# Batch 0's attention planned in halves of the heads, with its inputs in one row of the SyncE queue

## The chip, the cores and the metric

The kernel runs on one core of a Trainium2 chip. The metric is the device time of one execution in microseconds (us), the median of several runs. The engines are named as in the profile: PE (TensorE, with PEld for its weight loads), DVE (VectorE), ACT (ScalarE), POOL (GpSimd) and SP (SyncE, which only issues DMAs here).

## The reference

Two stages follow each other: a linear attention with cosine weights over 8 batches of 8 heads, 576 positions and 64 features, and a two-layer MLP with squared ReLU over the 4608 tokens that come out.

```python
# q, k, v: (8, 8, 576, 64) float32; w_in: (512, 2048); w_out: (2048, 512)
def phi(x, c, s):                     # c, s: cos and sin of pi/2 * pos / 576
    r = np.maximum(x, 0.0)
    return np.concatenate([r * c, r * s], axis=-1)
kv  = np.einsum('bhsf,bhsd->bhfd', phi(k), v)
z   = np.sum(phi(k), axis=2)
num = np.einsum('bhsf,bhfd->bhsd', phi(q), kv)
den = np.einsum('bhsf,bhf->bhs', phi(q), z)[..., None] + 1e-06
x   = (num / den).transpose(0, 2, 1, 3).reshape(4608, 512)
r   = np.maximum(x @ w_in, 0.0)
out = (r * r) @ w_out
```

## The kernel before

**Tiling.** A batch's 576 positions are four tiles of 128 (j = 0 to 3, the main part, with position p * 4 + j in row p) and a tail of 64. The tails of two batches share a tile, and the eight tails make a ninth block of 512 tokens for the MLP. All matmuls are in bf16. For one batch the attention does this: features of k (relu times cos, relu times sin, L320 on ACT or L324 on DVE), a cast of v into `vext` with a column of ones (L342, L344), the products of k and v summed over the tiles into `abank` (L366), a copy to `kvz` (L377); features of q, their transposes (L399 on PE, or a transposing DMA), a copy to `qpTp` (L407), the products with `kvz` (L418), a division in three DVE instructions (L436, L439, L442) into `x`, its transpose (L464 and the copy L468, or a DMA) into `xT`. The MLP's first matmul reads `xT` and `w1sb` into a PSUM bank, ACT takes the relu to `gT`, DVE squares it, and the second matmul reads `gT` and `w2sb`. Batches 0, 1 and 2 use plain products there (first matmul at L628 for batch 0, L487 and L503 for 1 and 2; second at L653 and L667), the later ones a form with seven products of halves instead of eight (L580, L766). `FIRST_7 = 3` says from which batch the first matmul has that form.

**Order.** Every instruction behind the opening is put into a `Plan`: an operation has an engine (or a choice of two), a cost, keys that it reads and writes, and a due time. `order` walks through modelled time, takes on each engine the ready operation with the earliest due time, and that order is the program. The table `SHIFTS` moves the due time of the operation with that number by so many microseconds. `plan.given` holds the times at which the plan takes data to be there.

**The opening before.** The opening is written out by hand ahead of the plan. SP issues the main part of k (1 MB). POOL issues k's tail, v (1 MB) and its tail, q in two pieces of two tiles each, and the four column blocks of w1, each cast from float32 (1 MB read) to bf16; a DMA that casts is issued on POOL. PE meanwhile runs 31 fillers on zeros (`warm`, L348). Then come k's features, v's casts, all products of k and v, one copy to `kvz`, tiles 0 and 1 of q through to `xT` with seven more fillers in the waits, q's features of tiles 2 and 3, and the loads for batch 1 (q, k, v) between the four blocks of w2, on POOL. The plan starts with the transposes of tiles 2 and 3 (L399 again). Batch 0's first matmul has eight parts: part s covers half s // 4 of the tokens (tiles 0 and 1, or 2 and 3) and column block s % 4 of w1, so parts 0 to 3 run through the four blocks for the first half, and 4 to 7 for the second.

Of the kernel before, what the change touches and what calls it, by code (L numbers as in the profile page):

```python
# [15 lines left out]
FP = 512  # L16
# [135 lines left out]
def kernel(  # L152
# [193 lines left out]
    def warm(n, banks):  # L346
        for i in range(n):
            nc.tensor.matmul(  # L348
                out=bank[banks[i % len(banks)]][:, :],
# [6 lines left out]
    def att_kv(b, js):  # L356
        vx, vxt = vexts[b % 2][0], vexts[b // 2 % 2][1]
        for j in js:
            for hh in range(HH):
                for half in range(2):  # L360
# [11 lines left out]
                    )  # L372

# [248 lines left out]
    def first_mm(s, step, a):  # L622
        half, hq = s // 4, s % 4
        for c in range(0, W, step):
            for i in (2 * a, 2 * a + 1):
                hb = hq * 4 + i
                for kb in range(KB):
                    nc.tensor.matmul(  # L628
                        out=bank[2 * (s % 2) + i // 2][:, i % 2 * W + c : i % 2 * W + c + step],
# [6 lines left out]
    def first_relu(s, a):  # L636
# [3 lines left out]
            in_=bank[2 * (s % 2) + a][:, :].rearrange("p (n c) -> p n c", n=2),  # L640
# [214 lines left out]
    def plan_q(b, j, cos=None, sin=None):  # L855
# [309 lines left out]
    for i, at in enumerate((16.4, 19.9, 22.6, 25.2)):  # L1165
        plan.given["w1", i] = at
# [29 lines left out]
    for s in range(8):  # L1196
        plan_first(s)
# [165 lines left out]
```

## Time and profile before

| what | us |
|---|---|
| median of 3 runs (lowest to highest) | 277.68 (277.61 to 278.15) |
| profiled execution, own time | 277.98 |
| its span, first to last instruction | 276.2 |
| PE busy (share of the span) | 265.8 (96%) |
| DVE busy | 216.5 (78%) |
| ACT busy | 186.4 (67%) |
| first matmul of batch 0's MLP (L628) | 19.67 |
| first matmul of batch 1's MLP (L487) | 54.26 |
| mean granted clock of PE | 0.996 |

The profile is one execution, so single durations belong to 277.98 us and not to the median. A PE that the profile calls busy need not run at its peak: the ends of matmuls are modelled. DMA rows are called q1 (issued on SP) and q0 (issued on POOL); all rows of a core share 16 DMA engines. A DMA share is the summed time of the packets over that of 16 engines, and goes over 1 in busy stretches.

### The profile page before, as it was taken

The page shows a single profiled execution, that of the slowest core. Times are in us where ns is not written, and L with a number is a line of the kernel's source. Part 1 is how long each engine was busy: PE and PEld are TensorE (multiplying, and loading weights), DVE is VectorE, ACT ScalarE, POOL GpSimd, SP SyncE. Part 2 cuts the span into 40 slices and gives each one's busy share as a digit, 9 for nine tenths or more (in the row PEclk, how much of TensorE's full clock was granted, in tenths as well). Part 3 has the DMA queues.
Part 4 walks back from the last instruction along what each step waited for, and adds up shares of the span by engine and source line. Part 5 has one row for each costly group of instructions (what it writes and reads, how often), then busy time and mean ns, then how long its engine had stood idle before and what let it go on. Part 6 is the DMA issues. An engine that isn't in the chain of part 4 may idle for free.

```text
span 276.2 us, 6556 instructions
## 1 busy us (share of the span) xinstructions
PE 265.8 (96%) x2651; PEld 210.5 (76%) x2659; DVE 216.5 (78%) x429; ACT 186.4 (67%) x334; POOL 19.3 (7%) x33
## 2 busy tenths in 40 slices
PE   8689999999999999999999999999999999999992
PEld 3368856665455459899888898999888888888882
DVE  1576695967965899799999998988999688967711
ACT  3575861796956698669998899957645665654131
POOL 8417100000000000000000000000000000000013
PEclk9999999999999999999999999999999999999998
DMA  7999998999999999998999999693033000300234
GB/s 210 319 207 278 311 253 268 291 219 351 225 253 282 252 214 217 316 304 197 245 283 236 261 264 326 118 232 103 14 59 128 26 4 0 141 13 2 81 112 114
DMA packets 83470, 53.38 MB, mean 193 GB/s; under 512 B 55888, under 2 KB 79824, under 8 KB 83440
## 3 DMA queue, kind: packets, MB, share of 16 engines
q1 hardware_dynamic: 77312, 42.28, 61.1%
q0 software_dynamic: 6048, 10.62, 16.3%
q8 instruction: 21, 0.34, 0.5%
q10 hardware_dynamic: 80, 0.07, 0.1%
q14 instruction: 9, 0.07, 0.1%
HBM read 36.70 MB, written 9.44 MB: 167 GB/s over the span
## 4 chain that ended last, share of the span: by engine, by line
PE 89%; DMA 3%; ACT 2%; DVE 2%; POOL 1%; issue 1%; POOLq 0%
PE bank L766 31%; PE bank L580 27%; PE bank L503 9%; PE bank L653 5%; PE bank L667 5%; PE bank L628 4%; PE abank L366 3%; PE abank L418 3%; DMA q<-in_q_dram 3%; ACT qp L320 1%; PE bank L399 1%; PE bank L487 1%; ACT gT L638 1%; DVE x L442 1%; PE bank L464 0%
## 5 line engine op out<-in xcount | busy, mean ns | idle before, releaser
L766 PEld LDWEIGHTS <-gT 128*128 128x128 bf16 x448 | 43.5, 98 | 5.1
L520 DVE TENSOR_TENSOR gT<-gT 128x2048 bf16<-128x2048 bf16 (+1 forms) x32 | 37.9, 1187 | 7.2 <-ACT gT L596 4.0
L766 PE MATMUL bank<-w2sb,gT 128*128 128x256 bf16 x336 | 42.2, 273 | 0.0
L580 PE MATMUL bank<-xT,w1sb 128*128 128x256 bf16 x288 | 41.1, 273 | 0.0
L580 PEld LDWEIGHTS <-w1sb 128*128 128x128 bf16 x384 | 36.9, 98 | 4.5
L596 ACT ACTIVATE gT<-bank 128x512 bf16<-128x512 f32 x48 | 28.8, 605 | 14.4 <-PE bank L580 14.1
L603 DVE TENSOR_TENSOR gT<-bank,qpTp 128x512 bf16<-128x512 f32 x48 | 31.0, 684 | 6.0 <-PE bank L580 5.9
L766 PEld LDWEIGHTS <-gs 128*128 128x128 bf16 x336 | 32.4, 98 | 3.7
L976 ACT COPY bank<-bank 128x512 f32<-128x512 f32 x48 | 27.9, 591 | 5.8 <-PE bank L580 5.2
L580 PEld LDWEIGHTS <-w1t 128*128 128x128 bf16 x288 | 27.7, 98 | 3.7
L580 PE MATMUL bank<-qpTp,w1t 128*128 128x256 bf16 x192 | 28.3, 273 | 0.0
L766 PE MATMUL bank<-w2t,gs 128*128 128x256 bf16 x224 | 28.2, 273 | 0.0
L503 PE MATMUL bank<-xT,w1sb 128*128 128x512 bf16 x116 | 27.7, 379 | 0.0
L512 ACT ACTIVATE gT<-bank 128x512 bf16<-128x512 f32 x32 | 18.6, 596 | 10.2 <-PE bank L503 10.1
L442 DVE TENSOR_TENSOR x<-abank,rden 128x512 bf16<-128x512 f32 x31 | 21.4, 692 | 1.1
L700 POOL DMA_DIRECT2D out_dram<-ysb x4 | 2.4, 615 | 239.6 <-ACT ysb L1068 236.7
L503 PEld LDWEIGHTS <-w1sb 128*128 128x128 bf16 x116 | 10.7, 98 | 11.0
L993 ACT COPY qpTp<-bank 128x512 f32<-128x512 f32 x24 | 14.0, 593 | 5.3 <-DVE x L442 2.5
L1064 DVE TENSOR_TENSOR ysb<-bank,y 128x512 f32<-128x512 f32 x14 | 9.6, 686 | 8.2 <-ACT y L1081 7.5
L320 ACT ACTIVATE kp<-k,sin_col 128x512 bf16<-128x512 f32 x21 | 14.6, 727 | 1.7 <-DMA k<-in_k_dram 1.7
L628 PE MATMUL bank<-xT,w1sb 128*128 128x256 bf16 (+1 forms) x160 | 15.4, 251 | 0.1
L436 DVE TENSOR_SCALAR den<-abank 128x8 f32<-128x8 f32 x35 | 5.6, 160 | 12.3 <-PE abank L418 12.3
(108 smaller groups left out, 445.7 us busy)
## 6 DMA issues: line engine op xcount, KB each, us to landing
out_dram<-ysb SPq DMA_DIRECT2D x16, 512.0 KB, 3.3
v<-in_v_dram SPq DMA_DIRECT2D x12, 512.0 KB, 7.2
q<-in_q_dram SPq DMA_DIRECT2D x12, 512.0 KB, 6.1
k<-in_k_dram SPq DMA_DIRECT2D x12, 512.0 KB, 6.5
v<-in_v_dram POOLq DMA_DIRECT2D x2, 1024.0 KB, 12.7
w1sb<-in_moe_w_in_dram POOLq DMA_DIRECT2D x4, 512.0 KB, 13.1
w2sb<-in_moe_w_out_dram POOLq DMA_DIRECT2D x4, 512.0 KB, 15.3
k<-in_k_dram SPq DMA_DIRECT2D x1, 1024.0 KB, 5.5
```

What stands on the lines that cost most here:

```text
L320: eng.activation(out=dst[ps, :, lo : lo + D], in_=src[ps], func=ACTF.Relu, scale=col[ps])
L442: nc.vector.tensor_tensor(out=x[:, a:z], in0=n4[:, :, :, 0:D].rearrange("p b (k l) d -> p b k l d", l=2), in1=rden[:, a:z] .rearrange("p b ...
L503: nc.tensor.matmul(out=out_, lhsT=w1sb[:, kb, hb * P : (hb + 1) * P], rhs=x_block(m, kb), start=(kb == 0), stop=(kb == KB - 1),)
L512: nc.scalar.activation(out=gT_of(m)[:, hb, :], in_=bank[to][:, :], func=ACTF.Relu)
L520: nc.vector.tensor_tensor(out=g, in0=g, in1=g, op=ALU.mult)
L580: nc.tensor.matmul(out=bank[to][:, s * W : (s + 1) * W], lhsT=lhs[:, kb, (2 * u + s) * P : (2 * u + s + 1) * P], rhs=rhs[:, kb, :], start= ...
L596: nc.scalar.activation(out=g_pair(m, i, j, u), in_=bank[to][:, :].rearrange("p (s c) -> p s c", s=2), func=ACTF.Relu,)
L603: nc.vector.tensor_tensor(out=g_pair(m, i, j, u), in0=bank[to][:, :].rearrange("p (s c) -> p s c", s=2), in1=in_five(u).rearrange("p (s c) ...
L628: nc.tensor.matmul(out=bank[2 * (s % 2) + i // 2][:, i % 2 * W + c : i % 2 * W + c + step], lhsT=w1sb[:, kb, hb * P : (hb + 1) * P], rhs=x ...
L766: nc.tensor.matmul(out=bank[to][:, s * DM2 : (s + 1) * DM2], lhsT=lhs[:, hb, s * P : (s + 1) * P], rhs=rhs[:, hb, :], start=(fresh and hb ...
L976: add("ACT", psum, lambda: nc.scalar.copy(out=bank[b][:, :], in_=bank[a][:, :]), r=[("bank", a)], w=[("bank", b)])
L993: add("ACT", psum, lambda u=u, Y=Y: nc.scalar.copy(out=in_five(u), in_=bank[Y][:, :]), r=[("bank", Y)], w=five)
```

## The change

The opening written by hand goes, and the plan now orders it. SP issues all of batch 0's inputs one behind the other: k, its tail, q's tiles 0 and 1, v's heads 0 to 3, v's tail, v's heads 4 to 7, q's tiles 2 and 3. On POOL a small copy out of v's first half (`gate`) stands ahead of the four w1 loads, so these are issued when that half has landed. The products of k and v, the copy to `kvz`, the products with q and the division of tiles 0 and 1 are done for heads 0 to 3 and heads 4 to 7 apart, each half in a bank of its own (`first_v`, `first_kv`, `first_kvz`, `first_num`, `first_div`). Batch 0's eight parts of the first matmul run in the order 0, 4, 1, 5, 2, 6, 3, 7. The fillers are 28 at the start and 10 single ones that the plan spreads; they write `abank` instead of banks 0 to 5. The table `SHIFTS` is another one, for the operations' new numbers. The few words that came with the change also name batch 2's first matmul as plain; no line of the diff speaks of it, and `FIRST_7` is 3 on both sides.

```diff
 SHIFTS = {
-    24: 2.4, 27: 4.4, 38: 2, 45: -2, 70: 2.6, 72: -12, 103: 8.6, 108: -11.2, 111: -8.8, 124: 1.2,
...
+    43: 1.2, 45: -4.2, 49: 2.2, 74: -0.2, 100: -1.6, 121: -1.2, 147: 3, 153: -2.6, 154: -5.4,
...
 }
...
+    def load_tiles(nm, b, eng, js):
+        kqv[nm, b] = main = home(inp, [P, H, J, D], nm, dtype=F32)
+        eng.dma_start(
+            out=main[:, :, js, :],
+            in_=src_of[nm][b, :, 0:MAIN, :].rearrange("h (p j) d -> p h j d", j=J)[:, :, js, :],
+        )
+
+    def gate():
+
+        got = home(const, [P, 1], "got", dtype=F32)
+        nc.gpsimd.tensor_copy(out=got[:, :], in_=kqv["v", 0][:, 0, 0, 0:1])
...
+    def first_kv(half, js):
+        vx, vxt = vexts[0]
+        for j in js:
+            for hh in range(HH):
+                h = half * HH + hh
+                if j < J:
+                    lhsT, rhs = kp_of(0, j)[:, h, :], vx[:, j, h, :]
+                else:
+                    lhsT, rhs = kp_of(0, j)[rows(0), h, :], vxt[rows(0), h, :]
+                nc.tensor.matmul(
+                    out=bank[4 + half][:, hh * E1 : (hh + 1) * E1],
...
+    def first_num(j, half):
+        for hh in range(HH):
+            nc.tensor.matmul(
+                out=bank[2 * j + half][:, hh * E1 : (hh + 1) * E1],
+                lhsT=qpTs[0, j][half][:, hh, :],
+                rhs=kvzs[0][:, half * HH + hh, :],
...
+    FIRST_S = (0, 4, 1, 5, 2, 6, 3, 7)
...
-    T0 = 16.8
-
-    for i, at in enumerate((16.4, 19.9, 22.6, 25.2)):
-        plan.given["w1", i] = at
+    T0, TM = 1.2, 15.4
+
+    for key, at in (
+        (("k", 0), 5.9), (("k", 1), 5.9), (("kt", 0), 6.3), (("q01",), 7.9), (("v", 0), 9.4),
+        (("vt", 0), 9.8), (("v", 1), 11.2),
+        (("q23",), 12.7),
+    ):
+        plan.given[key] = at
...
+    add("PE", 8.0, lambda: warm(28), w=[("T",)], due=0.0)
+    for i in range(10):
+        add("PE", 0.216, lambda: warm(1), w=[("T",)], due=20.0, after=9.2 + 0.5 * i)
+    add("POOL", 0.1, gate, r=[("v", 0)], due=0.0)
+    plan_pool(2.6, lambda: load_w1(0, 4), [("w1", 0)])
+    for i in range(1, 4):
+        plan_pool(2.6, lambda i=i: load_w1(i, 4), [("w1", i)])
...
-    for s in range(8):
+    for s in FIRST_S:
         plan_first(s)
...
     with tc.manual_schedule():
         load_main("k", 0, nc.sync)
-        load_tail("k", 0, nc.gpsimd)
-        load_main("v", 0, nc.gpsimd)
-        load_tail("v", 0, nc.gpsimd)
+        load_tail("k", 0, nc.sync)
+        load_tiles("q", 0, nc.sync, slice(0, 2))
+        load_half("v", 0, nc.sync, 0)
+        load_tail("v", 0, nc.sync)
+        load_half("v", 0, nc.sync, 1)
+        load_tiles("q", 0, nc.sync, slice(2, 4))
         constants()
-        load_main("q", 0, nc.gpsimd, 2)
-        warm(31, (0, 1, 2, 3))
...
         plan.run(T0)
```

More of the change, by code (lines that the diff above doesn't have):

```diff
@@ L344, in att_v, with warm @@
             copy(out=vexts[b // 2 % 2][1][ps, :, 0:D], in_=piece("v", b, j)[ps])
-    def warm(n, banks):
+    def warm(n):
         for i in range(n):
             nc.tensor.matmul(
-                out=bank[banks[i % len(banks)]][:, :],
+                out=abank[:, i % 2, :],
                 lhsT=zeros[:, 0:P],
@@ L372, in att_kv, with first_v @@
                     )
+    def first_v(half, js, eng):
+        hs = slice(half * HH, (half + 1) * HH)
+        copy = eng.copy if eng is nc.scalar else eng.tensor_copy
+        copy(
+            out=vexts[0][0][:, js, hs, 0:D],
+            in_=kqv["v", 0][:, hs, js, :].rearrange("p h j d -> p j h d"),
+        )
+    def first_kv(half, js):
[9 more added lines that the diff above has]
+                    out=bank[4 + half][:, hh * E1 : (hh + 1) * E1],
+                    lhsT=lhsT,
+                    rhs=rhs,
+                    start=(j == 0 and hh == 0),
+                    stop=(j == J and hh == HH - 1),
+                )
@@ new lines, in first_kvz @@
+    def first_kvz(half, eng):
+        kvzs[0] = home(att, [P, H, E1], "kvz", 0)
+        copy = eng.copy if eng is nc.scalar else eng.tensor_copy
+        copy(
+            out=kvzs[0][:, half * HH : (half + 1) * HH, :].rearrange("p h e -> p (h e)"),
+            in_=bank[4 + half][:, 0 : HH * E1],
+        )
+    def first_num(j, half):
[4 more added lines that the diff above has]
+                rhs=kvzs[0][:, half * HH + hh, :],
+                start=True,
+                stop=True,
+            )
@@ new lines @@
+    for j in range(2):
+        plan_q(0, j, src=[("q01",)])
+        plan_qT_pe(0, j, j, 10.0 + 0.3 * j, "DVE" if j == 0 else "ACT")
+    for half in range(2):
+        for i, e in enumerate(("DVE", "ACT")):
+            js = slice(2 * i, 2 * i + 2)
+            add(e, cost(e, FP, "cast"), lambda half=half, js=js, e=e: first_v(half, js, ENG[e]),
+                r=[("v", half)], w=[("v0", half, i)])
+        if half == 0:
+            plan_v(0, J)
+        for js, r in (
+            (range(J), [("v0", half, i) for i in range(2)] + [("kp", j, x) for j in range(J) for x in "cs"]),
+            ((J,), [("kpt", 0, "c"), ("kpt", 0, "s"), ("vt", 0, 0)]),
+        ):
+            add("PE", 0.135 * len(js), lambda half=half, js=js: first_kv(half, js), r=r, w=[("bank", 4 + half)],
+                due=11.0 + half)
+        add_either(260, "psum", lambda e, half=half: first_kvz(half, e), [("bank", 4 + half)], [("kvz", 0, half)])
@@ L1191 @@
+    for j in range(2):
+        for half in range(2):
+            add("PE", 0.14, lambda j=j, half=half: first_num(j, half), r=[where[0, j], ("kvz", 0, half)],
+                w=[("bank", 2 * j + half)], due=12.5 + 0.3 * j)
+            add("DVE", 0.65, lambda j=j, half=half: first_div(j, half), r=[("bank", 2 * j + half)], w=[("x", j)])
+        plan_x_pe(0, j, 4 + j, TM - 0.5 + 0.9 * j, "ACT")
     for j in (2, 3):
-        plan_qT_pe(0, j, 4 + j % 2, T0 + 1.0 + 0.4 * (j - 2), "DVE" if j == 2 else "ACT")
+        plan_q(0, j, src=[("q23",)])
+        plan_qT_pe(0, j, 4 + j % 2, TM - 1.0 + 0.4 * (j - 2), "DVE" if j == 2 else "ACT")
@@ L1193 @@
+    for i in range(2):
+        add("PE", 0.0, lambda: None, r=[("kvz", 0, i)], w=[("kvz", 0)])
     for j in (2, 3):
-        plan_num(0, j, T0 + 3.0 + 1.6 * (j - 2))
-        plan_x_pe(0, j, 4 + j % 2, T0 + 5.0 + 1.6 * (j - 2), "DVE")
-    for s in range(8):
+        plan_num(0, j, TM + 0.5 + 0.8 * (j - 2))
+        plan_x_pe(0, j, 4 + j % 2, TM + 1.8 + 0.8 * (j - 2), "DVE")
+    plan_pool(2.6, lambda: load_main("q", 1, nc.gpsimd), [("q", 0), ("q", 1), ("q01",), ("q23",)])
+    plan_pool(2.6, lambda: load_w2(0, 4), [("w2", 0)])
```

104 lines of the change are left out of this document (45 added, 59 removed), and 63 rows, old and new, of the table SHIFTS.

## The prediction, made before the changed kernel was run

> **What bounds the kernel now.** I read the page first, then busy time by stage, then the order of time of the first 55 us, then the DMA rows.
>
> ```profile
> span 276.2 us, 6556 instructions
> ...
> PE 265.8 (96%) x2651; PEld 210.5 (76%) x2659; DVE 216.5 (78%) x429; ACT 186.4 (67%) x334; POOL 19.3 (7%) x33
> ```
>
> TensorE is the engine that fills the span. By stage (columns: stretch, its length, busy time and count on each engine, granted clock, DMA share, GB/s):
>
> ```profile
> 0.00:6.40 6.40, 5.20 (x17) 2.08 (x18) 0.51 (x6) 1.71 (x4) 5.04 (x14) 1.00 0.71 209
> 6.40:12.20 5.80, 3.26 (x16) 1.37 (x14) 2.78 (x7) 3.60 (x6) 3.59 (x5) 1.00 0.98 330
> 12.20:19.60 7.40, 6.48 (x102) 4.91 (x103) 6.34 (x19) 5.07 (x9) 0.02 (x1) 1.00 1.23 217
> ...
> 54.00:271.20 217.20, 216.99 (x2154) 177.05 (x2156) 181.98 (x343) 154.91 (x282) 2.52 (x5) 1.00 0.72 175
> ```
>
> From 54 us on PE is busy 216.99 of 217.20 us at a clock of 1.00: no order of that work can save more than 0.2 us. The time to be had lies before PE's dense stream, whose first real matmul is the first one of L628. In order of time:
>
> ```profile
> 11.74 1.10 DVE L342 CAST vext<-v 128x512 bf16<-128x512 f32 x3 [3.02 <-DMA v<-in_v_dram]
> 12.23 1.13 PE L366 MATMUL abank<-vext,kp 128*128 128x65 bf16 x32 [2.57 <-DVE vext L342]
> ...
> 18.78 1.05 PE L399 MATMUL bank<-ident,qp 128*128 128x128 bf16 x16 [0.20 <-DVE qp L324]
> ...
> 19.67 1.06 PE L628 MATMUL bank<-xT,w1sb 128*128 128x128 bf16 x16
> ...
> 24.18 0.41 DVE L468 COPY xT<-bank 128x512 bf16<-128x512 bf16 x1
> ...
> 24.75 0.43 DVE L468 COPY xT<-bank 128x512 bf16<-128x512 bf16 x1 [0.16 <-PE bank L464]
> ```
>
> Batch 0's k is there at 6.37 us, but v's casts wait until 11.74 and PE's first product with them. The stream begins at 19.67 and ends at 271.1; 5.1 us of last copies and stores follow, which the change leaves alone. The DMA rows (packets, MB, share of the 16 engines): first 5.0 to 5.75 us, where both rows run, then 44.5 to 49.5 us, where the SyncE row runs alone.
>
> ```profile
> q0 software_dynamic: 49, 0.16, 81.4%
> q1 hardware_dynamic: 134, 0.12, 46.7%
> ```
> ```profile
> DMA packets 2002, 1.91 MB, mean 381 GB/s; under 512 B 169, under 2 KB 2002, under 8 KB 2002
> ...
> q1 hardware_dynamic: 2002, 1.91, 108.8%
> ```
>
> Alone, the SyncE row moves 381 GB/s. Between 5.5 and 7.0 us, where the GpSimd row takes over from it, the stage table gives 234 GB/s. The first chunk of w1, issued at 6.64, lands 10.6 us later (the w1sb tile's own view), at 17.26; the next ones each 2.5 to 2.6 us after (0.5 MB in bf16, 1 MB read).
>
> **Part by part. (1) The inputs in one SyncE row.** Seven issues take 0.4 to 1.0 us each on SP (rows of the later loads: half of v 0.4 to 1.0, vt 0.7 to 1.1), all before their data's turn. k lands as now, 5.5 us after 0.74, at 6.2. Behind it come, at 381 GB/s, kt 0.13 MB, q's tiles 0-1 0.52, half of v 0.52, vt 0.13, the other half 0.52, q's tiles 2-3 0.52: landings at 6.6, 7.9, 9.3, 9.7, 11.0 and 12.4. q's pieces are now 512 B long, and no row shows such pieces on this queue; by the 234 GB/s of the handover v's second half would land at 14.0, as late as q now. I take 11.0 to 12.0: the long stretch alone on the row is nearest. Today v lands at 11.7 and q's first tiles at 13.4, so q's features leave the critical place and v's halves take it.
>
> **(2) The gate and w1.** A copy of 128x1 on GpSimd (0.10 us, as its constants) waits for v's first half; queued behind it on GpSimd are all four w1 loads and after them q1, w2, k1 and v1. w1's first issue goes from 6.64 to about 9.4. That costs nothing while the input row keeps the DMA engines full (until about 11.5, 0.9 before the last landing); without that cover it would cost the idle time between, up to 2 us. With the engines never idle, w1's first chunk ends 2.6 us after the inputs: 15.0. Unchanged it would be 17.26. Both are the bounds.
>
> The Trainium skill (Trainium Kernel Development and Optimization, Key Constraints) says that the DMAs of all issuing queues run on the same 16 engines, and that spreading them saves issue time alone. By it the same bytes end when they did, w1 stays at 17.26, and the gain below shrinks by 0.9 us. The rates of 234 and 381 GB/s in this trace speak against a plain sum of bytes.
>
> **(3) The chain in halves.** From v's second half: cast 0.62 (ACT), 20 products (half of 1.13 + 0.41 us) 0.8, kvz half of 0.69, four products 0.2, division 0.1 + 0.20 + 0.38, transposes 0.39, ACT copy 0.58: 3.6 us, and six hand-overs of 0.2: 4.8. Landing at 11.0 to 12.0 gives xT's first tile at 15.8 to 16.8. DVE and ACT together: features of five k tiles and two q tiles at 0.48 + 0.71, casts 2.5, kvz 0.7, copies of qT 1.7, divisions 2.7, copies of xT 1.2: 17.1 us on two engines, from 6.3, so not before 14.9. Of weights (15.0 to 17.3), chain and load the middle of the first two decides: I take 16.5 for the first matmul of L628, against 19.67. Gain 3.17.
>
> **(4) What slides behind the start.** The sixteen transposes of q's tiles 2-3 at 18.78 ran before the stream, and now within it: 0.90 lost. The products and transposes of tiles 2-3 were already within it.
>
> **(5) The new order of the first matmul, 0, 4, 1, 5...** Part 0 is 32 matmuls of 56 ns, 1.8 us, to 18.3; transposes and products of tile 2 carry PE to 19.5. Part 4 needs xT of tile 2, part 1 w1's second chunk (17.6 at the earliest, 19.86 as now). Tile 2, from q's last landing: features 0.71, transposes 0.61, copy 0.69, products 0.41, division 1.06, transposes 0.39, copy 0.41: 4.3, and seven hand-overs of 0.2: 5.7. q's last piece (12.4 alone) shares the DMA engines with w1: at equal shares 13.8. So tile 2 is there at 19.5 and tile 3 some 1.3 later, while the first half of part 4 lasts 0.9. Bounds: nothing, if part 1 fills it, to 4 us (rival D). I take 0.9, less the 0.40 gap that PE has now at 23.8: 0.5 lost. In return each w1 chunk serves two parts, 3.7 us of PE against 2.6 us of DMA, so later chunks are not waited for.
>
> **(6) Warm-up, table, the rest.** 31 + 8 fillers become 28 + 10, all in time in which PE waits (2.57 us before L366): nothing, and if they came late, 0.2 us each on the chain. The clock stayed at 1.00 through that wait. The new table reorders everything behind; PE's 0.2 us of slack bounds its gain, 1.5 us (a wait like the longest now, 2.57, once, half covered) its loss; I take nothing. Supply behind: w2's first chunk lands at 30.5 and is used at 35.0, batch 2's xT lands at 74.0 and is used at 76.5; a stream 1.8 us earlier stays inside. "Batch 2's first matmul plain" is no part of the diff: FIRST_7 is 3 on both sides. Nothing.
>
> **Sum.** The profiled execution took 277.98 (span 276.2 and 1.78 around it): -3.17 + 0.90 + 0.50 = -1.77, so 276.2; the median of the runs is 0.30 lower: 275.9. My case runs from 275.0 to 277.0 (start 15.6 to 17.6).
>
> **Rivals.** B, everything packs: first matmul at 15.6, no new gap and the 0.40 one gone: -4.07 + 0.90 - 0.40, 274.1. For it: PE's stream has work enough. Against: DVE and ACT would have to be full from 6.3 on.
>
> C, given back: the same bytes end when they do now (what the Key Constraints quoted above would give). w1's first chunk stays at 17.26, the start gains 2.3 only, and batch 1's inputs come no earlier (v1 lands at 39.3 now, its xT serves PE at 54.3), since the GpSimd row already runs without pause (DMA share 1.15 from 19.6 to 35). PE starts early and waits before batch 1's first matmul: 277.7. Against: the faster row, above; w2 and v1 follow w1.
>
> D, slower: the second half of xT comes late. Today q's last piece lands at 14.8, and its xT copies end at 24.6 and 25.2, 9.8 us later. Behind part 0 nothing hides this any more: from 13.8 it gives 23.6, PE stands from 19.5 for 4.1 us: -3.17 + 0.90 + 4.1 = +1.8, 279.5. It decides from 21.8 on. Against: now nobody is in a hurry for them.
>
> E, q's last piece starved: if rows took turns packet by packet, its 64 packets of 512 B on each engine would each wait for one of the other row (means from the page's DMA table: 16.3% and 61.1% of 16 x 276.2 us over 6048 and 77312 packets, 119 and 35 ns): 9.9 us from its turn at 10.1, landing at 20.9, tile 2 at 26.6, PE 7.1 late: 282.5. Such turns are what the Trainium skill describes (DMA: Bandwidth & Descriptors, Queues, rings and completion order: round-robin between rows by packet). The trace agrees in part: at 5.0 to 5.75 us the SyncE row got 134 packets to 49, about equal bytes.
>
> **Numbers.** About 0.2% (0.56 us) is what a measurement of this kernel tells from no change. My case 0.53, B 0.13: faster 0.66. C 0.11: same. D 0.17 and E 0.06: slower 0.23. The range, 273.9 to 279.6, takes in B, C and D and leaves out E and the ends.
>
> **What would show it.** First matmul of L628's form at 16 to 17; v's casts at 9.4 and 11.2; w1's first landing at 15 to 16.5; a gap under 1 us before xT's second half; L503's first use 1 to 3 us earlier than 55.1; PE full from there. Wrong, if the first matmul is early and the first use of L503 is not, or if PE stands over 2 us after part 0.

## The result, and the profile after

The changed kernel takes 282.76 us (median of 4 runs, 281.76 to 283.02), the kernel before on the same chip 277.81: ratio 1.017 (1.0143 to 1.0198). It is slower by 4.95 us, where 1.8 less had been forecast. Run again beside another set of runs of before it took 281.13 against 277.24: 1.0147 (1.0101 to 1.0194). The two profiled executions (282.87 and 277.98) differ by 4.9 us, and 3.6 of these lie in the span; the time around the span was 3.07 us instead of 1.78 in that execution and 1.81 when the kernel was run again, so 1.3 us of this difference are no matter of the order of work.

From the page of the changed kernel:

```profile
span 279.8 us, 6568 instructions
...
PE 268.1 (96%) x2651; PEld 210.8 (75%) x2658; DVE 223.0 (80%) x446; ACT 179.2 (64%) x320; POOL 15.4 (6%) x29
...
PE 74%; DMA 15%; issue 4%; DVE 2%; ACT 1%; POOL 1%; POOLq 0%; SPq 0%; ACTq 0%
```

The last line is the chain that ended last, by engine. In the kernel before it is 89% PE and 3% DMA. So over some seventh of the span the work that ended last is now traced back to transfers, while PE itself is as busy as before beside them (96%). The stage table says where (same columns as for before):

```profile
0.00:6.40 6.40, 5.21 (x13) 1.90 (x14) 0.51 (x6) 1.68 (x3) 1.04 (x9) 1.00 0.75 199
6.40:12.20 5.80, 5.40 (x49) 2.92 (x48) 3.77 (x9) 4.82 (x8) 0.90 (x2) 1.00 1.16 244
12.20:19.60 7.40, 5.21 (x71) 3.38 (x70) 5.58 (x18) 4.06 (x7) 4.32 (x7) 1.00 1.21 240
19.60:35.00 15.40, 15.27 (x202) 14.03 (x200) 10.65 (x22) 10.49 (x18) 5.62 (x7) 1.00 1.18 264
35.00:54.00 19.00, 17.74 (x166) 10.73 (x167) 14.14 (x33) 7.22 (x13) 0.00 (x0) 1.00 1.13 289
```

From 6.4 to 12.2 us the DMA engines are busier than before (1.16 against 0.98) and move less (244 GB/s against 330). From 35 to 54 us PE stands 1.26 us, before 0.26. The milestones, read from the order of time ("run again" is the changed kernel's second profiled execution, of 280.91 us):

| start of | before | after | later by | run again |
|---|---|---|---|---|
| first matmul of batch 0's MLP (L628, now L702) | 19.67 | 20.38 | 0.71 | 19.68 |
| first matmul of batch 1's (L487, now L558) | 54.26 | 55.82 | 1.56 | 55.24 |
| first matmul of L580's form, now L651 | 97.55 | 98.75 | 1.20 | 98.07 |
| the last matmul | 271.03 | 274.62 | 3.59 | 274.01 |

So the opening is late by 0.7 us where 3.2 less had been forecast, and the dense stream behind it is 2.9 us longer. Run again, the kernel started level with before, and its stream was as long (254.3 us): the longer stream is the loss that both executions show, and the gain of the start is missing in both. The landings, against what the forecast said:

| tile | before | forecast | after | run again |
|---|---|---|---|---|
| k's tail | 6.92 | 6.6 | 7.83 | 7.53 |
| q's tiles 0-1 | 13.42 | 7.9 | 9.36 | 9.15 |
| v's first half | 11.72 | 9.3 | 11.25 | 11.18 |
| v's tail | 12.44 | 9.7 | 12.36 | 11.81 |
| v's second half | 11.72 | 11.0 to 12.0 | 13.69 | 13.20 |
| q's tiles 2-3 | 14.80 | 12.4 to 13.8 | 15.44 | 14.91 |
| w1, first chunk | 17.26 | 15.0 | 17.75 | 17.54 |
| batch 1's v | 39.27 | "follows w1" | 42.35 | 41.76 |

The second half of v decides over the chain, and it comes 1.97 us later than the whole of v did before. (In the other runs below with before's queues and with the tails the whole of v landed at 10.82 to 11.31, so 11.72 is late for these queues.) The row as SP issues it (start, duration):

```profile
2.71 2.25 SPq L229 DMA_DIRECT2D v<-in_v_dram  x1
5.00 1.25 SPq L239 DMA_DIRECT2D vt<-in_v_dram  x1
6.29 1.05 SPq L229 DMA_DIRECT2D v<-in_v_dram  x1
7.39 0.93 SPq L216 DMA_DIRECT2D q<-in_q_dram  x1
```

and stretches of one microsecond on the DMA engines (the last two numbers of a row are DMA share and GB/s):

```profile
6.00:7.00 1.00, 1.00 (x5) 0.36 (x4) 0.21 (x1) 0.24 (x1) 0.00 (x0) 1.00 1.28 159
...
9.00:10.00 1.00, 1.00 (x5) 0.29 (x3) 0.86 (x3) 0.94 (x2) 0.00 (x0) 1.00 1.11 336
...
11.00:12.00 1.00, 0.69 (x16) 0.56 (x14) 0.43 (x1) 0.73 (x2) 0.70 (x2) 1.00 1.09 162
```

One issue took 2.25 us (the prediction had 0.4 to 1.0 for its like), but all are out by 8.3. The rate falls to 159 and 162 GB/s around the tails: k's lands 1.15 us behind k (7.83 - 6.68) and v's 1.11 behind v's first half, 0.13 MB each, which at 381 GB/s is 0.34. In between the row reaches 336. The packets from 10 to 11 us, and then from 11 to 12, tell more exactly what is slow:

```profile
DMA packets 524, 0.23 MB, mean 228 GB/s; under 512 B 394, under 2 KB 524, under 8 KB 524
...
DMA packets 158, 0.16 MB, mean 162 GB/s; under 512 B 0, under 2 KB 158, under 8 KB 158
```

The tail's 256 B pieces move for the most part in the first stretch. The lowest rate is in the second, which has none of them: there the pieces of v's second half behind the tail take 110 ns each (a share of 1.09 over 16 engines for 1 us, by 158). So a tail costs less by its own pieces than by what happens to those behind it.

Then the chain, in order of time:

```profile
13.71 0.62 ACT L388 CAST vext<-v 128x512 bf16<-128x512 f32 x1 [0.91 <-DMA v<-in_v_dram]
13.71 0.64 DVE L388 CAST vext<-v 128x512 bf16<-128x512 f32 x1 [0.31 <-DMA v<-in_v_dram]
14.27 0.41 DVE L413 CAST kvz<-bank 128x260 bf16<-128x260 f32 x1
14.73 0.41 PE L420 MATMUL bank<-kvz,qpTp 128*128 128x65 bf16 x8 [0.40 <-DVE kvz L413]
...
14.99 0.67 PE L402 MATMUL bank<-vext,kp 128*128 128x65 bf16 x16
...
16.55 0.42 DVE L413 CAST kvz<-bank 128x260 bf16<-128x260 f32 x1
...
18.24 0.40 PE L535 MATMUL bank<-ident,x 128*128 128x128 bf16 x4 [0.69 <-DVE x L435]
...
18.56 0.59 ACT L539 COPY xT<-bank 128x512 bf16<-128x512 bf16 x1 [1.15 <-PE bank L535]
...
19.20 1.34 PE L470 MATMUL bank<-ident,qp 128*128 128x128 bf16 x16
19.30 0.59 ACT L539 COPY xT<-bank 128x512 bf16<-128x512 bf16 x1 [0.15 <-PE bank L535]
...
20.38 0.39 PE L702 MATMUL bank<-xT,w1sb 128*128 128x128 bf16 x4
```

Half 0 gains little on half 1. Its products with v ended at 13.1, but its copy to `kvz` (14.27) stands on DVE behind the cast of half 1 (13.71), which waits for its DMA; half 1's products with v (14.99) stand on PE behind half 0's with q; half 1's copy (16.55) stands on DVE behind both divisions of half 0; and PE does the sixteen transposes of q's tiles 2-3 before the MLP's first matmul, as the kernel before did. From landing to first matmul: 6.7 us.

What waits later shows in the chain that ended last (start, duration, what) and, below it, in the order of time:

```profile
12.58 8.60 DMA w1sb<-in_moe_w_in_dram
21.90 20.45 DMA v<-in_v_dram
...
103.99 4.80 DMA qptT<-qpt
```
```profile
43.05 1.13 PE L377 MATMUL abank<-vext,kp 128*128 128x65 bf16 x32 [0.70 <-ACT vext L353]
```
```profile
130.38 0.43 DVE L633 TENSOR_TENSOR qpTp<-xT 128x512 bf16<-128x512 bf16 x1 [1.70 <-DMA xT<-x]
130.84 0.42 DVE L633 TENSOR_TENSOR qpTp<-xT,qpTp 128x512 bf16<-128x512 bf16 x1
130.86 0.60 PE L651 MATMUL bank<-qpTp,w1t 128*128 128x256 bf16 x4 [0.73 <-DVE qpTp L633]
```

Batch 1's v, last but a few on GpSimd's row, lands at 42.35, is cast, and PE stands for it. PE also stands at 108.8 (0.37 us for a transposing DMA) and at 130 (for `xT`, which another transposing DMA brings). From 104 to 140 us PE is busy 34.73 of 36.00 us at a DMA share of 1.16; before, 36.00 of 36.00 at 1.07. Whether these later waits are the inputs' lateness handed on, or come from transfers that are slower in themselves, is not shown.

### The profile page after: what moved, and what is told of

Its sections match the earlier page's. It is cut to its first block, busy times and chain, and to the rows that moved or that the text cites. A ratio compares the mean times of both kernels' runs of the same rounds, so it can differ in the third digit from the quotient of the medians.

```text
span 279.8 us, 6568 instructions
## 1 busy us (share of the span) xinstructions
PE 268.1 (96%) x2651; PEld 210.8 (75%) x2658; DVE 223.0 (80%) x446; ACT 179.2 (64%) x320; POOL 15.4 (6%) x29
## 4 chain that ended last, share of the span: by engine, by line
PE 74%; DMA 15%; issue 4%; DVE 2%; ACT 1%; POOL 1%; POOLq 0%; SPq 0%; ACTq 0%
PE bank L840 28%; PE bank L651 24%; DMA v<-in_v_dram 7%; PE bank L574 7%; PE bank L741 5%; PE bank L727 3%; DMA w1sb<-in_moe_w_in_dram 3%; PE abank L489 3%; PE abank L377 3%; DMA out_dram<-ysb 2%; DMA qptT<-qpt 2%; DMA vt<-in_v_dram 2%; PE bank L558 1%; ACT vext L353 1%; DVE gs L819 1%
## 5 line engine op out<-in xcount | busy, mean ns | idle before, releaser
L651 PE MATMUL bank<-xT,w1sb 128*128 128x256 bf16 x288 | 41.5, 273 | 0.0
L667 ACT ACTIVATE gT<-bank 128x512 bf16<-128x512 f32 x48 | 28.5, 609 | 19.7 <-PE bank L651 15.1
L651 PEld LDWEIGHTS <-w1sb 128*128 128x128 bf16 x384 | 36.5, 98 | 4.9 <-issue 0.3
L651 PEld LDWEIGHTS <-w1t 128*128 128x128 bf16 x288 | 27.8, 98 | 4.5 <-issue 0.9
L651 PE MATMUL bank<-qpTp,w1t 128*128 128x256 bf16 x192 | 28.0, 272 | 0.7 <-DVE qpTp L633 0.7
L583 ACT ACTIVATE gT<-bank 128x512 bf16<-128x512 f32 x32 | 18.3, 604 | 9.1 <-PE bank L574 9.1
L513 DVE TENSOR_TENSOR x<-abank,rden 128x512 bf16<-128x512 f32 x30 | 20.8, 692 | 1.0
L702 PE MATMUL bank<-xT,w1sb 128*128 128x256 bf16 (+1 forms) x160 | 15.5, 251 | 0.0
L727 PE MATMUL bank<-w2sb,gT 128*128 128x512 bf16 x61 | 15.0, 379 | 0.3 <-issue 0.2
L741 PE MATMUL bank<-w2sb,gT 128*128 128x512 bf16 x61 | 14.5, 379 | 0.2
## 6 DMA issues: line engine op xcount, KB each, us to landing
q<-in_q_dram POOLq DMA_DIRECT2D x1, 1024.0 KB, 11.5
```

The costliest lines, as they stand in the source:

```text
L513: nc.vector.tensor_tensor(out=x[:, a:z], in0=n4[:, :, :, 0:D].rearrange("p b (k l) d -> p b k l d", l=2), in1=rden[:, a:z] .rearrange("p b ...
L583: nc.scalar.activation(out=gT_of(m)[:, hb, :], in_=bank[to][:, :], func=ACTF.Relu)
L651: nc.tensor.matmul(out=bank[to][:, s * W : (s + 1) * W], lhsT=lhs[:, kb, (2 * u + s) * P : (2 * u + s + 1) * P], rhs=rhs[:, kb, :], start= ...
L667: nc.scalar.activation(out=g_pair(m, i, j, u), in_=bank[to][:, :].rearrange("p (s c) -> p s c", s=2), func=ACTF.Relu,)
L702: nc.tensor.matmul(out=bank[2 * (FIRST_S.index(s) % 2) + i // 2][:, i % 2 * W + c : i % 2 * W + c + step], lhsT=w1sb[:, kb, hb * P : (hb + ...
L727: nc.tensor.matmul(out=bank[FIRST_Y[tt]][:, :], lhsT=gT_of(0)[:, hb, tt * P : (tt + 1) * P], rhs=w2sb[:, hb, :], start=(hb == 0), stop=(hb ...
```

## The experiments

Each run was compared with runs of the kernel before on the same chip (medians 277.2 to 277.8). "Start" is the first matmul of batch 0's MLP, "stream" from there to the last matmul's start, in the profile; before has 19.67 and 251.4, the changed kernel 20.38 and 254.2 (run again 19.68 and 254.3). One kernel's start can differ by 0.7 us or more, then, and each "start" below is that of one execution.

**Inputs and plan apart.** Two kernels cross the parts: the change with before's input queues, and before with the new row and gate.

```diff
 # a_inputs_old: the changed kernel, with
-        load_tail("k", 0, nc.sync)
-        load_tiles("q", 0, nc.sync, slice(0, 2))
...
+        load_tail("k", 0, nc.gpsimd)
+        load_main("v", 0, nc.gpsimd)
+        load_tail("v", 0, nc.gpsimd)
...
+        load_main("q", 0, nc.gpsimd, 2)
-    add("POOL", 0.1, gate, r=[("v", 0)], due=0.0)
+    add("POOL", 0.1, lambda: None, r=[("v", 0)], due=0.0)
```

> The changed kernel with batch 0's inputs issued as before (k on SP; the tails, v and q in two pieces on GpSimd ahead of w1; the gate's place in the plan kept, without its copy). Plan, halves and table stay. Theory R (the row delivers late, and the loads behind the gate with it): w1's first chunk lands near 17.3 instead of 17.75 and v of batch 1 near 39.5 instead of 42.35, and the time falls from 282.8 to 278 to 280. Theory T (the order behind, with its new table, loses the time whatever the inputs do): 282 to 284, because the plan counts on q at 7.9 and v at 9.4, and now both come later.

> The kernel before with the change's input row alone: the seven loads in the row's order on SP, and the gate ahead of w1. Hand-written opening, order and table stay. Theory R: w1's chunks land some 1.5 us later and v of batch 1 some 3 us later, so 280 to 282. Theory T: within 0.6 us of 277.8, since v's and q's data come no later than PE's first use of them.

Measured: 282.29 (ratio 1.0178, 1.0162 to 1.0193) and 286.78 (1.0334, 1.0305 to 1.0364). The first is where theory T had it, the second beyond both theories. From the waits of PE (us in total, times, longest), the first kernel, then the second:

```profile
PE bank L470 <- ACT qp L331: 4.3, 1, 4.3
```
```profile
PE abank L378 <- DVE vext L354: 4.0, 1, 4.0
PE bank L592 <- DVE qpTp L574: 3.6, 2, 2.7
```

The changed plan takes q first; with the old queues q lands at 12.88, PE stands 4.3 us for it, and the stream starts at 24.74. The order before takes v first; with the new row v's second half lands at 13.43, and the stream starts at 22.41. Order and landing times belong together, so neither half alone says what it costs within the whole. One thing is seen all the same: where the start is as late as 24.74 the stream is dense, 251.0 us, as before's 251.4. The 2.9 us by which it is longer in the changed kernel are not work added to the stream; started 4 to 5 us earlier, it waits.

**The gate.** The copy that holds w1 back is left out.

```diff
-    add("POOL", 0.1, gate, r=[("v", 0)], due=0.0)
+    add("POOL", 0.1, lambda: None, r=[("v", 0)], due=0.0)
```

> The changed kernel without the gate's copy: w1's four loads are issued on GpSimd from about 2 us on and share the DMA engines with the row. Theory R in the form that the gate holds the GpSimd row back too long: w1's last chunk lands 1 to 2 us earlier than 26.5, v of batch 1 as well, 280 to 281.5. If the row itself is the cost (small pieces, 1.1 us for each tail), the sum of the bytes is unchanged, inputs come later by as much as w1 comes earlier: 283 to 286. Theory T: no change beyond 0.6 us.

Measured: 289.38 (1.0438, 1.0411 to 1.0465), start 31.61. This is beyond both ranges of the expectation. w1's first chunk lands at 11.71 and v's second half at 23.85 instead of 13.69. From 12 to 17 us both rows got equally many packets (packets, MB, share):

```profile
q0 software_dynamic: 671, 0.67, 78.8%
q1 hardware_dynamic: 668, 0.49, 40.2%
```

The rows take turns packet by packet, and the row with the smaller pieces moves less: this is rival E's mechanism, at the row that the gate protects. The stream behind the late start is dense again (251.0 us), so the loss is that of the start. This kernel needs the gate.

**The table.** `SHIFTS = {}` in the changed kernel, the same in before, and the changed kernel in the old order of parts (`FIRST_S = (0, 1, 2, 3, 4, 5, 6, 7)`) without table.

> The changed kernel with an empty table of order. Theory T says that this table is of no use or of harm at these arrival times: 281 to 284. If the table does its work and the loss is the row's, taking it away costs what such a table is worth: 285 to 290.

> The kernel before with an empty table of order, to set beside the changed one without its table (285.8, 3 to 4.7 us more than with it). If the change's structure is no worse and only its table fits less well: 286 to 290 here, so the table before was worth 9 us or more. If the structure is what costs: 281 to 283, about as much table gain as in the changed kernel.

> The changed kernel without its table and with the parts of the first matmul in their old order 0 to 7, so that the two orders are compared with no table that fits one of them. If the new order of parts is a gain (w1's chunks are asked for half as fast): 0.5 to 2 us slower than 285.8. If it costs, because part 4 waits for the second half of xT: 1 to 2 us faster.

Measured: 285.79 (1.032, 1.0287 to 1.0354), 279.59 (1.0073, 1.0045 to 1.0101) and 285.25 (1.0287, 1.0229 to 1.0344). The new table is worth 3.0 to 4.7 us to the changed kernel (against its two medians), the old one 2.3 to before, which is less than either case of the expectation. So the table is not the cause; it covers part of it. Without tables the difference is 6.2 us. The order of parts makes no difference that these intervals show.

**The tails, and the form of the row.** The changed kernel again as it is; with k's and v's tails of batch 0 issued on GpSimd; and, on top of that, q whole in its first half's place.

```diff
 # a_tails_pool
-        load_tail("k", 0, nc.sync)
+        load_tail("k", 0, nc.gpsimd)
...
-        load_tail("v", 0, nc.sync)
+        load_tail("v", 0, nc.gpsimd)
 # a_row_big, also
-        load_tiles("q", 0, nc.sync, slice(0, 2))
+        load_main("q", 0, nc.sync)
...
-        load_tiles("q", 0, nc.sync, slice(2, 4))
```

> The changed kernel once more, beside the next three on one chip. If its 282.8 is the program's, 281.5 to 283 and the same landings as in its first profile to 0.5 us: v's second half at 13.7, w1's last chunk at 26.5, v of batch 1 at 42.3. If the slow spells of the DMA engines in its first profile (33 and 39 to 40 us) were an accident of that execution, v of batch 1 lands near 40.5 and the time is 280 to 281.

> The changed kernel with the two tails of k and v issued on GpSimd (as before), all else in the row. If pieces of 256 B in the row are what makes the inputs late (1.1 us a tail against 0.34 by bytes), v's second half lands 1.5 us earlier, at 12.2, the GpSimd row after it as well, and the time is 280 to 281. If the row's bytes set the landings whatever the pieces, within 0.6 us of the changed kernel.

> The changed kernel with no small pieces in the row: tails on GpSimd, and q in one load of 1 KB pieces in the place of its first half, v's halves behind it. By 381 GB/s v's second half lands at 11.5 to 12; with it the time is 279.5 to 280.5 if late inputs and a late GpSimd row are the loss. If the plan's order is, its DVE order is still the same and v's first half now comes later: 282 to 284.

Measured: 281.13, 283.22 (1.0211, 1.0178 to 1.0243) and 282.66 (1.0209, 1.0168 to 1.025). The second is slower than both cases of its expectation, the third is where it was expected if the plan's order costs. v's second half landed at 13.20, 13.64 and 15.57, and the stream started at 19.68, 21.84 and 24.62. Beside the row the tails cost as much as within it: from 6 to 10 us the engines moved 182 GB/s. So it isn't the place in the queue that makes a tail dear. In the second kernel something else came in; its rows of 18 to 21 and 21.5 to 24.5 us (PE busy second, granted clock third from the end):

```profile
18.00:21.00 3.00, 1.82 (x25) 1.23 (x24) 2.05 (x8) 1.01 (x2) 1.81 (x3) 1.00 1.24 207
21.50:24.50 3.00, 3.00 (x32) 3.00 (x30) 0.69 (x1) 0.63 (x1) 2.69 (x5) 0.50 1.24 207
```

PE ran at half its clock for 3.4 us just behind the start, and had already done so from 11.5 to 14.5 us; the third kernel's was at 0.50 from 13 to 18.5, ahead of its start, and its stream took 251.3 us, as dense as before's. The changed kernel itself has a clock of 1.00 in all stages.

**The tails left out.** Next the tails of k and v were left out of batches 0 and 1, in the changed kernel and in before, and then of batch 0 alone, in the changed kernel; zeros, set by DVE, stand in their place.

```diff
 def load_tail(nm, b, eng):
...
+        if b < 2 and nm != "q":      # a_no_tails0: b == 0 only
+            if b == 0:
+                nc.vector.memset(t, 0.0)
+            return
```

> The changed kernel with the tails of k and v of batches 0 and 1 not loaded (zeros in their place, set by DVE at the start; all arithmetic stays): 0.5 MB in 256 B pieces less. Theory S (the changed kernel waits for data that comes late, and the tails are what slows the row and the GpSimd row: about 1 us each): v's second half lands at 11.5 to 12 instead of 13.2 to 13.7, v of batch 1 at 38 to 39, PE's stream starts at 18 to 18.5 without the waits at 42 and 130 us, and the time is 277 to 278.5. Theory O (the order of the plan, not data, is what costs): landings move, the time stays above 280.5.

> The kernel before with the same four tails left out. Theory S: its data already comes ahead of PE's use, so it gains at most the earlier start, 0.5 to 1 us: 276.3 to 277.4, and the gap between the two kernels shrinks from 4 us to 1 or 2. Theory O: both gain alike, and the gap stays near 4.

> The changed kernel with only batch 0's last 64 rows of k and v left out (zeros take their place); batch 1's stay. Leaving out both batches' gave 278.42 against 281.13 to 282.76 with all. If the input row's tails are what makes the row late and through it everything behind on the GpSimd row: v's second half lands at 11.1 to 11.4, the first matmul stays near 18.4, batch 1's v lands near 39.5, and the time is 278.8 to 279.6. If batch 1's tails, in the middle of the GpSimd row, are what costs: batch 1's v is still later than 41 and the time is 280.5 to 282. Forecast: 279.3.

Measured: 278.42 (1.0046, 1.0015 to 1.0076), 276.71 (0.997, 0.994 to 1.0) and 280.11 (1.0078, 1.0045 to 1.011). The changed kernel gains 2.7 to 4.3 us by it, before 0.6. In a_no_tails the row lands near the times that the forecast had with the tails in it: q's tiles 0-1 at 8.11, v's halves at 9.61 and 11.14, q's tiles 2-3 at 12.85, batch 1's v at 38.30. Batch 0's two tails alone give 1.0 to 2.6 of that (v's second half at 11.44, batch 1's v at 40.49, start 18.64), batch 1's two, in the middle of GpSimd's row, the other 1.7; the intervals of a_no_tails and a_no_tails0 overlap, so this division is less sure than the sum. I had put nearly all on batch 0's (279.3): too much.

But the start only goes from 20.38 to 18.43. From the order of time of a_no_tails (its line numbers are 4 higher):

```profile
11.16 0.43 DVE L392 CAST vext<-v 128x512 bf16<-128x512 f32 x1
...
14.60 0.42 DVE L417 CAST kvz<-bank 128x260 bf16<-128x260 f32 x1
...
17.25 1.34 PE L474 MATMUL bank<-ident,qp 128*128 128x128 bf16 x16
...
18.43 0.55 PE L706 MATMUL bank<-xT,w1sb 128*128 128x128 bf16 x7
```

With v's second half at 11.14 the first matmul comes 7.3 us later, the chain as the plan laid it. w1's first chunk lies ready at 15.73. The kernel before without tails starts at 16.90: 1.53 us earlier, and its median is 1.7 below. What is left when the tails are gone has the size of that later start. That it is the same is not shown: the stream of a_no_tails is 254.0 us in its profiled execution, the slowest of ten (280.25), and that of before without tails 252.8.

**Is GpSimd's row a bound?** A dead load of 1 MB between batch 1's q and w2 on GpSimd's row, in the kernel before.

```diff
+        for i in range(2):
+            nc.gpsimd.dma_start(out=y_of(0, i)..., in_=k[1, i * HH : (i + 1) * HH, 0:MAIN, :]...)
```

> The kernel before with 1 MB more to load on GpSimd, between q of batch 1 and w2 (k of batch 1 once more, into the output tiles, which are free until 54 us). Nothing reads it, and no engine's work changes; all later loads land some 2.7 us later. If the DMA engines are a second bound, and lateness in the GpSimd row is carried to the end, 279.5 to 281 (v of batch 1 at 42, PE waiting for it). If PE's stream alone sets the end, within 0.6 us of 277.4.

Measured: 279.37 (1.007, 1.0043 to 1.0097), 2.1 us slower. Batch 1's v lands at 41.55 instead of 39.27, and PE stands there too:

```profile
42.24 1.13 PE L366 MATMUL abank<-vext,kp 128*128 128x65 bf16 x32 [0.43 <-ACT vext L342]
```

So the row had no 2.3 us to spare in the kernel before: "supply behind stays inside" was wrong, and an input row that makes GpSimd's row late makes PE wait once more at batch 1. (This execution's opening, which is before's, started the stream at 18.71, 1.0 earlier than before's own.)

**The halves and the plan's clock.** Without table, so that the planner's own order shows: the halves undone from the products on (whole heads, as before); before's queues; the plan told of the landings that had been measured, and of the time of each load on GpSimd; queues and landings together; and these with the halves undone.

```diff
 # true landings, changed queues
-    T0, TM = 1.2, 15.4
+    T0, TM = 1.2, 17.4
...
-        (("k", 0), 5.9), (("k", 1), 5.9), (("kt", 0), 6.3), (("q01",), 7.9), (("v", 0), 9.4),
-        (("vt", 0), 9.8), (("v", 1), 11.2),
-        (("q23",), 12.7),
+        (("k", 0), 6.9), (("k", 1), 6.9), (("kt", 0), 7.6), (("q01",), 9.2), (("v", 0), 11.2),
+        (("vt", 0), 12.0), (("v", 1), 13.4),
+        (("q23",), 15.1),
...
-    pool = [12.0]
+    pool = [13.1]
...
```

> The changed kernel without its table, with the halves undone from the products of k and v on: one step of products for all heads, then both copies to kvz, one step of products with q and one division for each tile. Loads, casts, row and gate stay. If the halves cost (half 1 stands behind half 0's products and divisions on PE and DVE, 12 DVE instructions for 10): the first matmul of batch 0's MLP 0.5 to 1.5 us earlier than 19.0 and 283 to 285. If they are harmless and late data decides: 285 to 287.

> The changed kernel without its table, with batch 0's inputs on the two queues as before and no gate. If the row is the part that costs: 281 to 283. If the plan's order is, which takes q first and now gets it last (12.9): 285 to 288, with the first matmul near 22 to 25.

> The changed kernel without its table, with the plan told the landings that the profiles show (v's second half 13.4, w1 from 17.75, v of batch 1 at 41.8) in place of its own, which are 2 to 4 us early. If the early clock makes a wrong order, so that an engine stands before work whose data is late: 281 to 283.5. If the data is late for any order: 285 to 286.5.

> The same with batch 0's inputs on the two queues as before, no gate, and their landings told to the plan (v 11.1, q 12.9 and 14.3, w1 from 16.7, v of batch 1 at 39.2). What is left of the change are the halves, the order of the parts and the planned opening. If row and clock together are the loss: 279 to 280.5, level with the kernel before without its table (279.6). If the halves cost too: 281 to 283.

> The changed kernel without table, with before's input queues and the planner told of them, and with batch 0's attention put back to whole heads from the products on. The same kernel with the halves measured 281.52, before without its table 279.59, so 1.9 us are left between the two, and the first matmul of the MLP started at 19.68 there against 17.61. If the halves are what is left: 279.2 to 280.0, first matmul near 17.6. If the halves are harmless and the rest (the gate of w1, batch 2's first matmul plain) is what is left: 281.2 to 282.0, first matmul near 19.7. Forecast: 279.8, since the longer chain from v's second half to the first matmul was seen even where that half landed as early as had been planned (11.14 to 18.43).

| without table | us (ratio, 95%) | start | PE at half clock |
|---|---|---|---|
| the changed kernel | 285.79 (1.0287 to 1.0354) | 19.02 | 0 |
| halves undone | 287.24 (1.0316 to 1.0424) | 20.64 | 3.0 |
| before's queues | 285.05 (1.0235 to 1.0318) | 23.36 | none behind the start |
| true landings | 287.77 (1.0326 to 1.0432) | 18.69 | 3.3 |
| queues and landings | 281.52 (1.0098 to 1.0188) | 19.68 | 0 |
| these, halves undone | 282.48 (1.0123 to 1.0206) | 19.66 | 1.7 |
| before | 279.59 (1.0045 to 1.0101) | 17.61 | 0 |

(The last column is PE's busy time in the half-clock stretches of the profiled execution, in us, times one half; with the true landings a second stretch, at 130 us, is in it.) Before's queues alone gain 0.7 and the true landings alone lose 2.0, with intervals that overlap the changed kernel's; together they gain 4.3, with intervals apart. With the queues that it was told of, the plan loses little. The runs with the halves undone (287.24) and with the true landings came out slower than either case of their expectations; before's queues alone are where they were expected if the plan's order costs.

The last run decided about the halves. Undone, they leave the start where it was (19.66 against 19.68) and the time too, as far as the overlapping intervals tell (282.48 against 281.52). That is what was expected if the halves are harmless, and the forecast of 279.8 failed. From the landing of q's first tiles to the start it is 7.07 us without the halves and 6.62 with them. (In the changed queues the start even came later without them, 20.64 against 19.02; but there the clock was at 0.50 from 18 us on, so that pair says little.) So no run shows the halves to make the opening long. What does is seen beside before without table, where q's first tiles land as early (12.61 against 12.59) and the first matmul comes 2.05 us sooner. Before without table, then the last run:

```profile
14.04 0.84 DVE L374 COPY qpTp<-bank 128x512 bf16<-128x512 bf16 x2
14.07 1.20 ACT L374 COPY qpTp<-bank 128x512 bf16<-128x512 bf16 x2
...
17.61 0.61 PE L595 MATMUL bank<-xT,w1sb 128*128 128x128 bf16 x8
```
```profile
13.97 0.49 DVE L303 TENSOR_SCALAR qp<-q,sin_col 128x512 bf16<-128x512 f32 x1
...
14.77 0.68 DVE L446 COPY qpTp<-bank 128x1024 bf16<-128x1024 bf16 x1
...
15.35 0.99 ACT L446 COPY qpTp<-bank 128x1024 bf16<-128x1024 bf16 x1
...
19.00 0.61 PE L438 MATMUL bank<-ident,qp 128*128 128x128 bf16 x8 [0.67 <-ACT xT L507]
...
19.66 0.57 PE L670 MATMUL bank<-xT,w1sb 128*128 128x128 bf16 x4
```

The hand-written order copies q's transposes at once. The plan first does the features of tiles 2-3 on DVE and ACT (from 13.97 on), and it puts eight of those tiles' transposes (19.00) ahead of the MLP on PE. How the 2.05 us divide between these was not measured.

The clock came into the last run as well. Its rows of 15 to 19 and 20 to 23 us:

```profile
15.00:19.00 4.00, 1.52 (x22) 0.92 (x22) 2.69 (x11) 1.93 (x3) 3.26 (x5) 1.00 1.24 207
20.00:23.00 3.00, 3.00 (x35) 3.00 (x33) 1.34 (x4) 0.61 (x2) 1.40 (x2) 0.50 1.24 229
```

PE, 1.52 of 4 us busy, is put to half clock once the stream has begun. With the halves it was busy 1.99 of these 4 us, in before without table 3.59, and both kept 1.00. The Trainium skill (TensorE: Matmul & The Clock Gate, Part 1) describes this as a half rate that follows an idle window of about 3.4 us and ends after a busy one of that length. The length agrees (3.4 us at 0.50 here); but the window ahead of it was not idle. A low busy share is not the rule either: in a_tails_pool PE was busy 1.82 of 3.00 us just before its clock fell.

What a spell at half clock costs the whole kernel is not shown. The kernel with the halves undone and the changed queues took 287.10 and 287.17 in the two executions with a mean granted clock of 0.985 and 0.986, and 287.31 and 289.54 in the two with 0.997 and 0.998.

## Why the prediction was wrong

Against the forecast of 276.2 for the profiled execution, 282.87 is 6.7 us too much. Of these, 3.9 are the start (20.38 where 16.5 was taken), 1.5 the stream (2.9 us longer where steps 4 and 5 gave 1.4), and 1.3 lie around the span. Three steps failed: the row's rate (1), the chain (3) and the supply behind the start (6).

**Step 1, the row's rate, failed first.** The term was the bytes behind k at 381 GB/s, a rate taken from a stretch in which 169 of 2002 packets were under 512 B. From k's landing (6.68) to that of v's second half (13.69) the row moved 1.84 MB in 7.0 us, 262 GB/s. So v's second half came 1.7 us behind the later end of the range taken; the bound that was named and passed over, 14.0 at 234 GB/s, was nearer. Most of what was mis-sized is the tails: 0.34 us each was said, and without batch 0's two tails v's second half lands 1.8 to 2.3 us earlier (11.44 against 13.20 and 13.69). The rest of the row was mis-sized too: without any tails it moved the other 1.57 MB in 4.8 us (6.32 to 11.14), 326 GB/s.

**Step 2, the gate, failed with it.** The gate's copy took 0.44 us where 0.10 had been said. Its cover held, as the DMA engines' share was 1.09 to 1.28 in each microsecond from 5 to 13, but w1's first chunk ends 2.3 us after the inputs, at 17.75, since these end late. Rival C's 17.26 was closer. Nothing here speaks against the gate costing nothing, and without it 6.6 to 8.3 us are lost.

**Step 3, the chain, failed by itself.** 4.8 us were summed from durations and hand-overs; 6.7 passed, and 7.3 where the row landed as forecast. The sum followed one half through free engines. In the plan's order half 0's steps stand in front of half 1's on PE and DVE, four half divisions of 0.76 us cost DVE 3.0 where two whole ones cost 2.2, and PE does the transposes of q's tiles 2-3 before the MLP. The order is what lengthens the chain, and not the halves as such: with whole heads in the planned order the start was no earlier (19.66 against 19.68, both with before's queues and without tables). Of the gain of 3.17 nothing came: the start moved by +0.71, and by 0.01 when the kernel was run again.

**Step 4** put the transposes of q's tiles 2-3 into the stream at 0.90. They stay ahead of it (19.20), so they are part of the late start instead.

**Step 5** took 0.5 us too much. PE does not stand after part 0, which was its lower bound; rival D did not happen, and the old order of parts without table gives the same time.

**Step 6 failed in one sentence.** Warm-up and clock were nothing, as said. The new table brought no loss: it is worth 3.0 to 4.7 us to its kernel, the old one 2.3 to before, so by these differences it gained more than the 0.2 us that bounded it. But "supply behind" has no reserve: batch 1's v at 42.35 instead of 39.27 makes PE stand at 43, and the stream grows by 2.9 us in all, some 1.3 of it by waits between 104 and 140 us whose cause is open. Rival C saw that GpSimd's row runs without pause and took from it only that batch 1 would come no earlier; that it could come later, as the inputs ahead of it take more time on the same engines, was the case that was missing. The size (282.8) is near rival E's 282.5 by luck, as its place is another: q's last piece, which E starves, came at 15.44, and the tails with v's second half cost.

The account by the runs: of 3.9 to 4.95 us some 2.1 to 3.7 go with the tails of batches 0 and 1 (2.7 to 4.3 in the changed kernel less 0.6 in before), and 1.7 stay when they are gone. The planned opening, which at equal landings starts 2.05 us later than the hand-written one, is the likely source of these, but no run put the old opening into the changed kernel. Open are also the waits from 104 to 140 us.

## What to carry to other kernels

Before moving transfers into one row, sum each piece at the rate of its own kind, taken from a stretch that has such pieces: here two transfers of 256 B pieces set what stood behind them back by 1.8 to 2.3 us, where their bytes gave 0.7. Where an order was laid out for certain landing times, check it against landing times 2 us off, and set its chain beside that of the old order at equal landings: here the planned opening was 2.05 us longer. And look at who else uses the DMA engines in the next 40 us before calling a late row harmless: here the share of transfers in the chain that ended last went from 3% to 15%.

## What the runs showed of the hardware

- A load of 0.13 MB in 256 B pieces over 64 partitions landed 1.11 to 1.15 us behind the load ahead of it, 114 to 118 GB/s, in a row that reached 336 a few microseconds later. Issued on the other row beside it, it still held the whole to 182. The Trainium skill (DMA: Bandwidth & Descriptors, Specifications) puts the least piece for full rate at 512 B. The trace agrees in part: the 256 B pieces are dear, but mostly through the 1 KB pieces just behind them (110 ns each from 11 to 12 us, where without the tails 356 pieces took 49 ns each from 8.5 to 9.5), and in a_no_tails 512 B pieces moved 294 GB/s from 6 to 7 us, 1 KB pieces 349 from 8.5 to 9.5.
- With work in both rows (a_no_gate, 12 to 17 us) the rows got 671 and 668 packets: turns go by packets, not by bytes (0.67 and 0.49 MB).
- One SyncE issue took 2.25 us in a row of seven, where the three ahead of it took 0.47 to 0.74.
- PE's clock fell to 0.50 for 3.4 us after a stretch in which it was 38% busy, and in another run after one of 61%; it stayed at 1.00 after one of 50%. So the busy share of such a stretch does not tell it.
- 256 B packets of the SyncE row between 56 and 104 us took 26 ns in the mean in the changed kernel (26.5 without the tails), 28 in before with the new row, but 23 in before and 22 with the old queues. No experiment was made on why.
